# Writing out the opening of a spectral and gated kernel in a fixed order

## The chip, the cores and the metric

The kernel runs on one core of a Trainium2 chip. The metric is the device time of one execution, in microseconds (us). The kernel before was timed in three runs; their median is 1420.48 us (1419.91 to 1420.74). A difference of under 0.2% of that, 2.84 us, is about what a measurement of this kernel cannot tell from no change.

The engines are named as the profile names them: PE (matrix products and transposes), PEld (its weight loads), DVE (the vector engine), ACT (the scalar engine), POOL, and SP, whose queue issues most transfers. Each engine works off its own list of instructions strictly in order and waits for others at semaphores.

## The reference

The input is one activation of 2048 rows by 576 columns. A layer norm is taken over the columns; then the output is the sum of the input, a filter in the two-dimensional Fourier domain, and a gated linear unit:

```
xn = _layernorm(x, axis=-1)
return x + _A_ref(xn, A_w_r, A_w_i) + _B_ref(xn, B_w_gate, B_w_up, B_w_down)
```

where `_A_ref` is `irfft2(rfft2(x) * (w_r + i w_i))`, and `_B_ref` is `h = sigmoid(x @ w_gate) * (x @ w_up)` followed by `h @ w_down`. The gate and up matrices are 576 by 4608, the down matrix is 4608 by 576. This change touches only the first part of the gated unit: the layer norm of the first 1024 rows, their transposes, and the first few products with the gate and up weights.

## The kernel before, in words

**Number format.** [...] A product of 288 columns of depth is written as seven PE instructions (`STEPS`, L630, in `prod`, L634): for each of the two full 128-row pieces of the depth high×high, low×high and high×low, and one for the 32 columns that are left over, whose high, high and low copies are stacked in 96 rows. High parts are made on ACT by a copy, low parts on DVE by a subtraction.

**Tiling of the gated unit.** The 576 columns are two halves of 288, called 1 and 2. The rows are taken in two pairs of chunks of 512 rows; a chunk is four row tiles of 128. `A11`, `A12` are the two column halves of the first chunk of the pair, `A21`, `A22` those of the second; `XA` gives each its place in the tile `X`, which holds them transposed. The 4608 hidden columns are 36 units of 128. From the third unit on, `unit` computes both chunks with seven products in the manner of Strassen, out of sums of these blocks (`S1` to `S4`, made by `sums` and transposed by `fill`). The first two units, whose sums are not ready yet, are computed plainly: `plain(u, c)` (L648) is one call, for unit `u` and chunk `c`, with four products of seven instructions, two into a gate bank and two into an up bank. There are four such calls for the first pair of chunks, in the order (0,0), (1,0), (0,1), (1,1); below they are calls one to four.

**Banks.** The gate bank of unit 0 is called `A` and that of unit 1 `B`; each has one buffer, so call three cannot write bank `A` before the sigmoid of call one (L659) has read it. The up bank `E` has two buffers. Transposes go through `pair` tiles (tag `pp`, two buffers of two halves each).

**The layer norm.** `moments` (L356) takes mean and variance of a row tile on DVE. `scales` (L362) forms the reciprocal root: a square root on ACT, a reciprocal and one refining step in small DVE instructions of two to four columns. `prep_hi` (L405) writes the normalised row tile `xa` on ACT. `fill` (L431) transposes, for one block and two row tiles, the two full pieces and the left-over columns together (four and two PE instructions), copies both out of the bank on ACT (L443, L444), and subtracts for the low part on DVE (L445).

**What sets the order.** The program is built by a scheduler which puts each engine's instructions in order by the sequence of the code and its own estimate of when operands are ready. `placed` (L233) nails an instruction to the sequence of the code while `late_input` is set, which it is up to the end of call four. Side work stands in generators: `second_chunk` (L949) is the weights of unit 1 and the transposes of the second chunk, advanced a few steps at each turn of the plain calls and finished after call one.

**The opening before.** SP issues four row tiles, both halves of unit 0's weights, two row tiles, unit 1's weights, two row tiles (L877 to L880). Meanwhile PE multiplies an identity by itself (L892, L910), which computes nothing that is used. Then come the statistics and transposes of row tiles 0 and 1, those of 2 and 3, the weights of unit 0 (`make_p`, L274), and the statistics of the second chunk's four row tiles in one go (L919).

```
    for k in ("A11", "A12"):
        fill(0, k, 0)
    for n in range(4):
        tc.keep_in_program_order(nc.tensor.matmul(b0, idr, eye, start=False, stop=True, skip_group_check=True))
    for m in (2, 3):
        prep(0, m, 0)
    next(mk)
    next(mk)
    for k in ("A11", "A12"):
        fill(0, k, 1)
```

## Time and profile before

| what | value |
|---|---|
| median of three runs | 1420.48 us (1419.91 to 1420.74) |
| time of the profiled execution | 1421.62 us |
| its span, first to last instruction | 1419.8 us |
| PE busy | 1405.9 us, 99% of the span |
| DVE busy | 1112.5 us, 78% |
| ACT busy | 640.6 us, 45% |
| first product with real weights | 17.01 us after the start |
| first product with the down weights | 63.22 us after the start |

A row of the timeline gives start and length in us, engine, line, operation, what is written and what is read, and how many were merged; in brackets stand the idle time of the engine before it and what ended it. A length runs to the end of the last instruction's pipeline, so that the distance between the starts of two rows of PE is the better measure of PE's own time. PEclk is the clock granted to PE, 1.00 for the full one.

### The profile page before, as it was taken

Reading aid. Unit: us, or ns where it says so; the run is one execution under the profiler, and the core shown is the slowest. Engines: PE = TensorE matmul, PEld = TensorE weight load, DVE = VectorE, ACT = ScalarE, POOL = GpSimd, SP = SyncE. Lnnn points to the kernel's source line nnn. Section 1 sums busy time; section 2 is a strip of 40 time slices with the busy share of each in tenths; the row PEclk is TensorE's granted clock in tenths of the full one; section 3 lists DMA queues with packets and bytes.
Section 4 is the critical chain, followed back from the end, with each engine's and each line's share of the span. In section 5 each row is a group of like instructions: output and inputs, shape, how many; then the busy total and the mean of one; then the engine's idle time right before and its main releaser. Section 6 shows DMA issues by size and latency. Waiting matters only on the chain. (4 is left out here: it accounts for less than half of the span.)

```text
span 1419.8 us, 20725 instructions
## 1 busy us (share of the span) xinstructions
PE 1405.9 (99%) x7883; PEld 1235.9 (87%) x7883; DVE 1112.5 (78%) x1722; ACT 640.6 (45%) x1035; POOL 3.3 (0%) x5
## 2 busy tenths in 40 slices
PE   8999999999999999999999999999999999999998
PEld 6888888888888888888888888888888889999897
DVE  6988888888888888789466888877878877766784
ACT  5644444444444443444235444434545534434431
POOL 0000000000000000000000000000000000000000
PEclk9999999999999999999999999999999999999999
DMA  6498677777777776675767777778888787766643
GB/s 250 181 329 308 256 267 262 270 263 270 263 269 263 269 263 247 242 254 176 270 217 234 224 234 223 217 245 267 275 269 272 236 290 221 247 215 204 195 126 84
DMA packets 130899, 343.10 MB, mean 242 GB/s; under 512 B 12176, under 2 KB 51632, under 8 KB 125936
## 3 DMA queue, kind: packets, MB, share of 16 engines
q1 hardware_dynamic: 129872, 340.47, 71.0%
q8 instruction: 62, 1.02, 0.3%
q10 hardware_dynamic: 928, 1.31, 0.3%
q14 instruction: 37, 0.30, 0.1%
HBM read 205.60 MB, written 136.13 MB: 241 GB/s over the span
## 5 line engine op out<-in xcount | busy, mean ns | idle before, releaser
L636 PE MATMUL pB<-X,w 128*128 128x512 f32 x1484 | 379.9, 393 | 0.0
L636 PEld LDWEIGHTS pB<-X,w 128*128 128x128 f32 x1484 | 268.0, 188 | 49.6 <-ACT v L700 1.3
L636 PE MATMUL pE<-X,w 128*128 128x512 f32 x1064 | 271.8, 392 | 0.5 <-DVE y L701 0.5
L636 PE MATMUL pA<-X,w 128*128 128x512 f32 x1008 | 261.4, 395 | 1.2 <-DVE X L445 0.8
L636 PEld LDWEIGHTS pE<-X,w 128*128 128x128 f32 x1064 | 193.2, 188 | 35.4 <-DVE y L701 1.0
L636 PEld LDWEIGHTS pA<-X,w 128*128 128x128 f32 x1008 | 184.5, 190 | 35.4 <-DVE X L445 1.7
L743 PE MATMUL po<-wd,hh 128*128 128x288 f32 x1216 | 210.8, 295 | 0.0
L834 PEld LDWEIGHTS ps<-wf,hs 128*128 128x128 f32 x1260 | 188.9, 188 | 17.9 <-ACT qs L842 0.9
L834 PE MATMUL ps<-wf,hs 128*128 128x288 f32 x1260 | 202.0, 295 | 0.4 <-ACT qs L842 0.4
L743 PEld LDWEIGHTS po<-wd,hh 128*128 128x128 f32 x1216 | 184.2, 188 | 11.8 <-ACT hh L726 0.4
L747 DVE TENSOR_TENSOR acc<-acc,po 128x576 f32<-128x576 f32 x168 | 125.7, 749 | 67.3 <-PE po L743 66.8
L240 ACT ACTIVATE w<-raw 128x768 fp32r<-128x768 f32 (+1 forms) x106 | 100.8, 952 | 93.1 <-PE pE L636 36.5
L743 PE MATMUL po<-wd,hl 128*128 128x288 f32 x608 | 128.7, 293 | 0.0
L844 DVE TENSOR_TENSOR qs<-qs,ps 128x576 f32<-128x576 f32 x112 | 84.1, 751 | 28.4 <-PE ps L834 27.4
L743 PEld LDWEIGHTS po<-wd,hl 128*128 128x128 f32 x608 | 98.7, 189 | 0.0
L701 DVE TENSOR_TENSOR y<-v,pE 128x512 f32<-128x512 f32 x68 | 46.7, 686 | 52.2 <-ACT v L700 51.3
L844 DVE TENSOR_TENSOR acc<-acc,ps 128x576 f32<-128x576 f32 x90 | 67.5, 750 | 23.3 <-PE ps L834 22.6
L242 DVE TENSOR_TENSOR w<-raw,w 128x512 fp32r<-128x512 f32 (+1 forms) x106 | 81.8, 772 | 3.2 <-ACT w L240 2.9
L721 DVE TENSOR_TENSOR y<-y,g 128x1024 f32<-128x1024 f32 x67 | 81.9, 1222 | 3.1
L770 ACT ACTIVATE hs<-y 128x512 fp32r<-128x512 f32 x105 | 64.8, 628 | 38.2 <-DVE y L721 14.6
L704 ACT ACTIVATE g<-pB 128x512 f32<-128x512 f32 x68 | 40.7, 598 | 89.9 <-PE pB L636 89.9
L700 ACT ACTIVATE v<-pB 128x512 f32<-128x512 f32 x68 | 40.6, 598 | 71.0 <-PE pB L636 70.7
(175 smaller groups left out, 1609.0 us busy)
## 6 DMA issues: line engine op xcount, KB each, us to landing
w<-wsp SPq DMA_DIRECT2D x246, 320.0 KB, 3.5
wsp<-w SPq DMA_DIRECT2D x34, 2240.0 KB, 7.8
raw<-in_w SPq DMA_DIRECT2D x34, 768.0 KB, 9.7
wdsp<-wd SPq DMA_DIRECT2D x36, 576.0 KB, 4.6
wf<-tsp SPq DMA_DIRECT2D x60, 288.0 KB, 3.9
wf<-wdsp SPq DMA_DIRECT2D x45, 288.0 KB, 3.9
std<-in_wd SPq DMA_DIRECT2D x36, 288.0 KB, 5.5
ri<-in_ri SPq DMA_DIRECT2D x16, 578.0 KB, 5.3
```

The source lines that it names most:

```text
L240: placed(nc.scalar.activation(o[:, :, :3, :], src, AF.Copy))
L242: placed(nc.vector.tensor_tensor(o[:, :, 3:, :], src[:, :, :KT, :], f32(o[:, :, :KT, :]), op=OP.subtract))
L636: nc.tensor.matmul(bank, w[:, sw, :], X[:, x, sx, :], start=start and j == 0, stop=stop and j == len(STEPS) - 1, skip_group_check=skip)
L700: nc.scalar.activation(v[:, 1], bank["B"], AF.Copy)
L701: nc.vector.tensor_tensor(y[:, 1], v[:, 1], bank["E"], op=OP.add)
L704: nc.scalar.activation(g[:, 1], bank["B"], AF.Sigmoid)
L721: nc.vector.tensor_tensor(y, y, g, op=OP.mult)
L743: nc.tensor.matmul(pd[:, b, :HD], h[i], w[k][b], start=g == 0 and n == 0, stop=g == G - 1 and n == 2)
L747: nc.vector.tensor_tensor(a, a, pd[:, :, :HD], op=OP.add)
L770: nc.scalar.activation(hs[:, 0], src, AF.Copy)
L834: nc.tensor.matmul(pd[:, i, :HD], h[:, a, m], w[:, b], start=q == 0, stop=q == 2)
L844: nc.vector.tensor_tensor(o, o, pd[:, :, :HD], op=OP.add)
```

## The change

The opening is written as one function, `opening`, which is called in place of plain calls one and two; nearly all its instructions are `placed`. It does the following.

- **Transfers.** The order on SP becomes two row tiles, the gate half of unit 0's weights, two row tiles, the up half, two row tiles, both halves of unit 1's weights, two row tiles.
- **Statistics.** The square root reads the variance itself and gets the small constant as its bias, so that one small DVE step before it and one after it go. The second chunk's statistics are taken two row tiles at a time, as the first chunk's are.
- **Weights first.** ACT copies the gate half of unit 0's weights ahead of the first normalised row tile.
- **Transposes apart.** The full pieces (`lift`) of `A11` and `A12` are transposed together for two row tiles. The left-over columns (`lift_rem`) of all four row tiles go later, four PE instructions for a block and one copy of 512 columns on ACT.
- **Left-overs last.** In calls one and three (`plain_late`) the six instructions of a product that need full pieces alone are issued first (`LOW_LAST`), and the four that need left-over columns stand at the end. The transposes of the left-over columns stand between.
- **Second chunk inside call two.** The row tiles of the second chunk are normalised and transposed between the products of call two.
- **Sigmoids.** The sigmoid of call one moves from the middle of call one to the end of call two, behind all square roots of the opening.
- **Identity products.** There are 15, then 10; before there were 21, ten of full height and eleven more of which eight are of half height in pairs, and then 4.

The new functions and the order, cut:

```diff
+    for todo in ((new_acc, 0, 0), (new_acc, 0, 1), (load_raw, 0, 2), (new_acc, 0, 2), (new_acc, 0, 3), (load_raw, 0, 0),
+                 (new_acc, 0, 4), (new_acc, 0, 5), (load_raw, 1, 2), (load_raw, 1, 0), (new_acc, 0, 6), (new_acc, 0, 7)):
+        todo[0](*todo[1:])
...
-        nc.vector.tensor_scalar(ve, mv[:, ts, 1], EPS, None, op0=OP.add)
         if table:
-            nc.scalar.activation(w0, ve, AF.Sqrt)
-            nc.vector.reciprocal(r0, w0)
+            placed(nc.scalar.activation(w1, mv[:, ts, 1], AF.Sqrt, bias=nmr[:, NT - 1:]))
+            placed(nc.vector.tensor_scalar(ve, mv[:, ts, 1], EPS, -0.5, op0=OP.add, op1=OP.mult))
+            placed(nc.vector.reciprocal(r0, w1))
...
+    def lift(k, mm, main):
+        for j in range(2):
+            for q in range(KT):
+                placed(nc.tensor.transpose(main[:, (2 * q + j) * P:(2 * q + j + 1) * P],
+                                           XS[2 * mm + j][:, XP[k], q * P:(q + 1) * P], idf))
+        v, o = main.rearrange("p (q s) -> p q s", q=KT), X[:, XA[k], :, 2 * mm * P:(2 * mm + 2) * P]
+        return (lambda: placed(nc.scalar.activation(o[:, :KT], v, AF.Copy)),
+                lambda: placed(nc.vector.tensor_tensor(o[:, KT + 1:], v, f32(o[:, :KT]), op=OP.subtract)))
+    def lift_rem(k, ms, rest, srcs=None):
+        for j, m in enumerate(ms):
+            src = srcs[j] if srcs else XR[m, XP[k]]
+            placed(nc.tensor.transpose(rest[:KR, j * P:(j + 1) * P].bitcast(F32R), src, idr))
+        o = X[:KR, XA[k], KT, ms[0] * P:(ms[-1] + 1) * P]
+        return lambda: placed(nc.scalar.activation(o, rest[:KR, :len(ms) * P], AF.Copy))
...
+    LOW_LAST = ((0, 0), (1, 1), (0, 3), (1, 4), (3, 0), (4, 1))
...
+    def plain_late(u, c, beside, mid):
+        G_, bank = new_plain(u, c)
...
+            prod(bank[b], *of_plain(u, c, b, k), k == 1, False, steps=LOW_LAST)
...
+                prod(bank[b], *of_plain(u, c, b, k), False, k == 2, steps=STEPS[-1:])
+            if b == 0 and (u, c) != (0, 0):
+                gate(G_, bank)
...
+    def opening():
...
+        identity(15)
+        scaled(0, 0)
+        early(0, 2)
+        level(0, 0)
+        scaled(0, 1)
+        p1 = pair("px_A11")
...
+        hi_and_lo("A11", 0, p1[:, 0], lows)
+        hi_and_lo("A12", 0, p2[0], lows)
+        identity(10)
+        level(0, 1)
...
+        first = plain_late(0, 0, lambda i: None, mid)
...
+        for k in (1, 2):
+            prod(bank[0], *of_plain(1, 0, 0, k), k == 1, k == 2)
+        lows = []
+        p4 = pair("px_A2_0")
+        for n, k in enumerate(("A21", "A22")):
+            hi_and_lo(k, 0, p4[:, n], lows)
+        scaled(1, 1)
+        level(1, 1)
...
+        p5 = pair("px_A2_1")
+        for n, k in enumerate(("A21", "A22")):
+            hi_and_lo(k, 1, p5[:, n], lows)
+        prod(bank[1], *of_plain(1, 0, 1, 2), False, True, steps=STEPS[4:])
...
+        for m in range(TPC):
+            rem_hi(m, 2, "rm34", TPC)
+            rem_lo(m, 2)
...
+        gate(*first)
+        plain_ends(0, 0, *first)
+        while ends:
+            end()
+        gate(G_, bank)
+        plain_ends(1, 0, G_, bank)
...
+            if p == 0 and n == 2:
+                plain_ends(u, c, *plain_late(u, c, beside, rest_of_second))
```

Three places show what this does to the order on the engines. In the rows `xa` is a normalised row tile, `raw` weights as loaded and `w` their parts, `px_` a bank with transposes, `rs` the small tiles of the statistics, `rm` and `rma` left-over columns, `pA`, `pB`, `pE` the banks of the plain calls, `g` a sigmoid, `y` and `hh` the product with it and its high part. A row says for which engine's semaphore it waits.

First, ACT at the start. Before, from the first square root on:

```order
L368 ACTIVATE rs0_230<-rs0_230 128x2 [waits DVE_49]
L410 ACTIVATE xa0_0_218<-acc_163,nmr_65,rstd_64 128x576 [waits DMAHW1_49,DVE_49,Activation_49]
L410 ACTIVATE xa0_1_219<-acc_163,nmr_65,rstd_64 128x576 [waits DMAHW3_49]
L392 ACTIVATE rma0_0_0_240<-xa0_0_218 128x2x64 [waits Activation_49]
L392 ACTIVATE rma0_1_0_243<-xa0_1_219 128x2x64 [waits Activation_49]
L368 ACTIVATE rs2_255<-rs2_255 128x2 [waits DVE_49]
```

The same place on ACT with the change:

```order
L356 ACTIVATE rs0_225<-mv_63,nmr_65 128x2 [waits DVE_49]
L241 ACTIVATE w0_200<-raw0_182 128x2x384 [waits DMAHW4_49]
L398 ACTIVATE xa0_196<-acc_163,nmr_65,rstd_64 128x576 [waits DMAHW1_49,DVE_49,Activation_49]
L398 ACTIVATE xa1_197<-acc_163,nmr_65,rstd_64 128x576 [waits DMAHW3_49]
L356 ACTIVATE rs2_244<-mv_63,nmr_65 128x2 [waits DVE_49]
```

The weights' copy, with its wait for a transfer, moved ahead of the first normalised row tile, and the left-over columns moved away from here.

Second, ACT around the sigmoid of call one. Before, from the square root of the second chunk:

```order
L368 ACTIVATE rs4_340<-rs4_340 128x4 [waits DVE_49]
L240 ACTIVATE w1_360<-raw1_189 128x2x384 [waits DMAHW2_49]
L659 ACT_TABLE_LOAD
L659 ACTIVATE g0_0_349<-pA0_0_351 128x512 [waits PE_49]
L240 ACTIVATE w1_360<-raw1_189 128x2x384 [waits DMAHW3_49]
L410 ACTIVATE xa0_0_218<-acc_163,nmr_65,rstd_64 128x576 [waits DMAHW0_49,DVE_49]
```

With the change, from the second square root of the second chunk:

```order
L356 ACTIVATE rs6_413<-mv_63,nmr_65 128x2 [waits DVE_49]
L398 ACTIVATE xa2_198<-acc_163,nmr_65,rstd_64 128x576 [waits DMAHW4_49,DVE_49]
L398 ACTIVATE xa3_199<-acc_163,nmr_65,rstd_64 128x576 [waits DMAHW5_49]
L418 ACTIVATE X_66<-px_A2_1_436 128x2x256 [waits PE_49] x2
L381 ACTIVATE rm340_2_452<-xa0_196 128x2x64 [waits Activation_49]
L381 ACTIVATE rm341_2_455<-xa1_197 128x2x64 [waits Activation_49]
L381 ACTIVATE rm342_2_458<-xa2_198 128x2x64 [waits Activation_49]
L381 ACTIVATE rm343_2_461<-xa3_199 128x2x64 [waits Activation_49]
L646 ACT_TABLE_LOAD
L646 ACTIVATE g0_0_308<-pA0_0_309 128x512
L652 ACTIVATE hh0_466<-y0_0_465 128x512 [waits DVE_49]
L646 ACTIVATE g1_0_355<-pB1_0_356 128x512
```

The table load and the sigmoid of call one moved from ahead of the second chunk's row tiles to behind them, their transposes' copies and four copies of left-over columns.

Third, PE from the second chunk's last transposes into call three. Before:

```order
L440 MATMUL px0_A22_1_438<-idr_62,rma0_2_2_421 96x128
L439 MATMUL px0_A22_1_438<-idf_61,xa0_3_221 128x128 x2
L440 MATMUL px0_A22_1_438<-idr_62,rma0_3_2_425 96x128
L636 MATMUL pA0_1_492<-X_66,w0_296 128x512 [waits Activation_49]
L636 MATMUL pE0_1_493<-X_66,w0_296 128x512
L636 MATMUL pA0_1_492<-X_66,w0_296 128x512 [waits DVE_49]
```

With the change:

```order
L415 MATMUL px_A2_1_436<-idf_61,xa3_199 128x128 [waits Activation_49]
L415 MATMUL px_A2_1_436<-idf_61,xa3_199 128x128
L415 MATMUL px_A2_1_436<-idf_61,xa2_198 128x128 [waits Activation_49]
L415 MATMUL px_A2_1_436<-idf_61,xa2_198 128x128
L415 MATMUL px_A2_1_436<-idf_61,xa3_199 128x128 x2
L627 MATMUL pE1_0_357<-X_66,w1_201 128x512 x3
L627 MATMUL pA0_1_479<-X_66,w0_200 128x512 [waits Activation_49]
```

The third row of these is the first transpose of `A22`: it writes the second half of the pair tile whose first half ACT is copying out, and waits for that copy. The wait of the last row is for the sigmoid of call one, which reads bank `A`. The four transposes for the left-over columns of `A21` and four for `A22` (tile `px_r2`) follow twelve instructions later, and those of `A22` in the same way wait for the copy of `A21`'s, which stands on ACT behind the sigmoids of calls one and two.

## The prediction

> **What bounds the kernel now.** I read the page's busy times first, then the stages of the opening as windows, then PE's, ACT's and DVE's timelines row by row.

> ```profile
> span 1419.8 us, 20725 instructions
> PE 1405.9 (99%) x7883; PEld 1235.9 (87%) x7883; DVE 1112.5 (78%) x1722; ACT 640.6 (45%) x1035; POOL 3.3 (0%) x5
> ```

> PE is busy but for 13.9 us in all (1419.8 - 1405.9). What follows the opening is the same work in before and after, and PE has no slack there that could swallow a delay: whatever the opening gains or loses on PE stays to the end. So I forecast when PE reaches one fixed point, the first product with the down weights. The windows, with busy times, then the granted clock, DMA share and GB/s, are those from the start to the first product, call one, call two, and calls three to six.

> ```profile
> 0.00:17.01 17.01, 11.48 (x49) 7.86 (x49) 8.58 (x34) 8.81 (x19) 3.29 (x5) 0.97 0.76 274
> 17.01:26.64 9.63, 9.19 (x29) 7.05 (x29) 8.57 (x27) 4.32 (x8) 0.00 (x0) 0.70 0.61 219
> 26.64:36.59 9.95, 9.61 (x55) 7.55 (x53) 8.66 (x22) 8.42 (x20) 0.00 (x0) 1.00 0.60 213
> 44.28:63.22 18.94, 18.49 (x101) 15.13 (x100) 18.05 (x33) 15.47 (x30) 0.00 (x0) 1.00 0.52 197
> ```

> The first holds 5.5 us without work for PE (17.01 - 11.48), and the second runs at a mean clock of 0.70. There is the gain to be had; call two has only 0.34 us of idle time to lose.

> ```profile
> 3.80 7.44 PE L892 MATMUL b<-idr 128*128 128x512 f32 x21 [3.80 <-DMA idr<-c_id]
> 11.08 0.60 PE L439 MATMUL px_A<-idf,xa 128*128 128x128 f32 x4
> ...
> 14.48 0.66 PE L439 MATMUL px_A<-idf,xa 128*128 128x128 f32 x4 [1.14 <-ACT xa L410]
> ...
> 17.01 0.79 PE L636 MATMUL pA<-X,w 128*128 128x512 f32 x1
> 18.24 5.38 PE L636 MATMUL pA<-X,w 128*128 128x512 f32 x13 [0.43 <-DVE X L445]
> 23.46 3.34 PE L636 MATMUL pE<-X,w 128*128 128x512 f32 x14
> 26.64 3.34 PE L636 MATMUL pB<-X,w 128*128 128x512 f32 x14
> ...
> 37.04 3.25 PE L636 MATMUL pA<-X,w 128*128 128x512 f32 x13 [0.37 <-DVE X L445]
> ...
> 41.49 0.38 PE L439 MATMUL px_S<-idf,xa 128*128 128x128 f32 x2
> 41.62 0.30 PE L440 MATMUL px_S<-idr,rma 128*96 128x128 f32 x1
> ...
> 44.28 3.40 PE L636 MATMUL pB<-X,w 128*128 128x512 f32 x14
> ...
> 55.49 0.44 PE L439 MATMUL px_S<-idf,xa 128*128 128x128 f32 x2 [0.45 <-DVE X L445]
> ```

> A product takes 0.227 us at full clock ((26.64 - 23.46) / 14) and 0.40 at half ((23.46 - 18.24) / 13, its last ones being faster). A transpose takes 0.065 ((41.62 - 41.49) / 2). Why the products from 18.24 are slow, stretches of 3.41 us show:

> ```profile
> 9.22:12.63 3.41, 3.41 (x23) 2.32 (x22) 1.51 (x11) 1.25 (x6) 0.00 (x0) 1.00 1.04 410
> 12.63:16.04 3.41, 1.72 (x12) 1.02 (x11) 1.80 (x4) 3.41 (x9) 0.00 (x0) 1.00 0.59 223
> 16.04:19.46 3.42, 2.94 (x11) 1.92 (x10) 3.05 (x5) 2.62 (x6) 0.00 (x0) 0.50 0.00 0
> 19.46:22.87 3.41, 3.41 (x10) 2.64 (x9) 3.27 (x11) 0.00 (x0) 0.00 (x0) 0.50 0.71 285
> 33.11:36.52 3.41, 3.07 (x20) 2.10 (x18) 3.41 (x10) 2.56 (x8) 0.00 (x0) 1.00 0.61 236
> ```

> One stretch at 50% busy (1.72 of 3.41) is followed by half clock; a stretch at 86% (2.94) did not bring it back, a full one did; one at 90% did not lower it. Half clock therefore came in portions of 3.41 us, at least two of them here.

> **The change, part by part.** The rows that carry the terms on ACT, DVE and the queues:

> ```profile
> 7.67 1.62 ACT L410 ACTIVATE xa<-acc,nmr,rstd 128x576 f32<-128x576 f32 x2 [1.07 <-DVE nmr L382]
> ...
> 12.06 0.60 ACT L443 ACTIVATE X<-px_A 128x512 fp32r<-128x512 f32 x1 [2.14 <-PE px_A L440]
> ...
> 15.47 0.84 ACT L240 ACTIVATE w<-raw 128x768 fp32r<-128x768 f32 x1
> ...
> 24.96 1.28 ACT L659 ACT_TABLE_LOAD   x1
> 26.25 0.60 ACT L659 ACTIVATE g<-pA 128x512 f32<-128x512 f32 x1
> ...
> 29.00 0.50 ACT L392 ACTIVATE rma<-xa 128x128 fp32r<-128x128 f32 x2
> ...
> 33.60 0.64 ACT L664 ACTIVATE hh<-y 128x512 fp32r<-128x512 f32 x1
> ...
> 49.69 0.85 ACT L240 ACTIVATE w<-raw 128x768 fp32r<-128x768 f32 x1 [1.38 <-DVE raw L264]
> ```

> ```profile
> 4.17 0.82 DVE L359 BATCH_NORM_STATS2 st<-acc 128x6 f32<-128x288 f32 x2 [3.30 <-DMA acc<-in_x]
> ...
> 6.63 0.17 DVE L369 RECIPROCAL rs<-rs 128x2 f32<-128x2 f32 x1 [0.27 <-ACT rs L368]
> ...
> 7.42 0.16 DVE L382 SCALAR_TENSOR_TENSOR nmr<-mv,rstd 128x2 f32<-128x2 f32 x1
> ...
> 26.91 0.69 DVE L663 TENSOR_TENSOR y<-g,pE 128x512 f32<-128x512 f32 x1 [0.65 <-ACT g L659]
> ```

> ```profile
> 0.74 1.83 SPq L348 DMA_DIRECT2D acc<-in_x  x4
> 2.62 0.91 SPq L228 DMA_DIRECT2D raw<-in_w  x2
> DMA to landing us min/median/max: 6.1/7.1/8.0
> ```

> *First product.* ACT's new copy of the gate weights stands ahead of the first normalised row tile and waits for a transfer. That is issued after two row tiles instead of four, at about 1.7 (0.74 + 1.83 / 2). If it lands in its own median of 7.1 it is there at 8.8; if it takes only as long as the first row tile, 3.43 us (4.17 - 0.74), at 5.1. With half as much ahead of it I take about 6.5: the copy (0.84) then ends by 7.4, when the scales are ready anyway (7.58 less one removed DVE step, 0.17). The normalising of two tiles (1.62) ends near 9.2; 15 identities at 0.35 (7.44 / 21) hold PE to about 9.8; eight transposes and two copies of 0.6 that overlap a little bring ACT to 11.45, the second two tiles to 13.07, their first transposes and copy the first product to 14.2. With the late landing everything is 1.1 later, 15.3. Before: 17.01.

> *Call one.* 28 products at 0.227 are 6.35; eight left-over transposes 0.6; the second four write the other half of the tile that ACT is copying out, so PE waits for a copy, 0.6 and its start, 0.85. 14.2 + 7.8 = 22.0 against 26.64: a lead of 4.6, of which some 2 is the half clock of before that a quicker start would avoid.

> *Call two* is where the lead goes. Its 28 products are 6.35 us for PE, but between them now stands a chain that PE, ACT and DVE pass to and fro. The gate half, 14 products, ends at 25.2. Then: transposes of `A21`, copy, transposes of `A22` (PE waits 0.85), copy, to 27.7; square root 0.2 and DVE's small steps 0.95 (6.63 to 7.58), to 28.85; two tiles normalised, 1.62, to 30.5; again transposes, copy, wait, transposes, copy, to 32.9; four left-over copies at 0.2 (0.50 less the pipeline's end, for two), to 33.65; the table load, 1.28, to 34.9; the sigmoid of call one, to 35.5. Call three's first product writes bank `A`, so it waits for that sigmoid: 35.55 instead of 36.59 (37.04 less two products). PE's last product of call two ends near 32.75, so the wait is 2.8 us, and the lead is down to 1.0. Before, the table load and the sigmoid lay beside call one's up products (24.96 and 26.25, against 23.46 to 26.64).

> *Call three.* Twelve products (2.7) and four transposes later, at 38.6, PE waits for ACT's copy of the first left-over tile, which stands behind `hh` of call one, the sigmoid of call two, a left-over copy and `hh` of call two: 0.69 + 0.64 + 0.60 + 0.3 + 0.69 + 0.64 + 0.6 = 4.2 after the sigmoid, at 39.9 with starts. That is 1.35 of waiting. 28 products, the left-overs' 0.6, the side transposes of some 1.1 and this wait put call four's start at 45.0; before it is 44.28. A lag of 0.7.

> *Calls four to six.* Up to 63.22 PE waits only 0.45 before. Now the last left-over part of the sums comes behind the copy of unit two's weights, which itself waited 1.38 for DVE before. So the additional wait is between -0.45 (none left) and 1.4; I take 1.0, nearest to the row of 1.38. Lag 1.7.

> *Clock.* From 29.4 to 35.5 PE has only three products and eight transposes, and is busy for about a quarter of the time. Wherever the stretches of 3.41 us lie, one falls into it wholly or nearly so, at well under the 50% that lowered the clock before. Half clock then begins between 32.8 and 36.2 and holds for two portions, 6.83 us. At most this loses 6.83 x (1 - 0.227 / 0.40) = 3.0; the 1.35 of waiting in call three hides part: 1.6 at least. I take 2.0.

> Costed at nothing: the later issues on SP (unit 1's weights and the spills of weight parts, which PE reaches long after; cover: call one), POOL, the left-over copies grouped in fewer (0.37 eight times to 0.6 four times, a gain of 0.6 on ACT that already stands in the times above), the identities, 25 instead of 25. If unit 1's weights came late, call two would begin later than 22.0, and the chain with it.

> Sum: 0.7 + 1.0 + 2.0 = 3.7 us. The profiled execution took 1421.62, 1.1 above the median of 1420.48; 1421.62 + 3.7 = 1425.3, and for the median 1424.2.

> **Rivals.** *The clock stays full:* 1.7 alone, 1422.2. For it: only one stretch in before shows the drop, and the long wait is 2.8 us, not a whole stretch. Against it: that one was half busy, and this is emptier. [...]

> *The clock also falls early,* between the transposes of the start or in call two's first group, where PE is about 75 to 80% busy, between the 50% that lowered it and the 90% that did not: another 2.3, since part of it lies beside waits: 1426.5.

> *Faster:* the sigmoid of call one is off the path. If the chain through call two runs 2.8 us quicker (left-over copies and table load in ACT's waits for PE, done by 32.75), call three starts with the products' end, the clock has no reason to fall and the lead of 3.8 stays but for call three's wait: 3.7 - 2.8 - 2.0 = -1.1. ACT's backlog there and in the calls after would be gone too, since it stems from the late sigmoid: without 1.35 and 1.0 it is -3.4, so 1417.1. To break even the sigmoid must be done near 33.8, with the clock up. Against it: on ACT the sigmoid stands behind all of the chain, each link of which has a row above.

> **How the numbers follow.** A measurement tells no less than 0.2%, 2.84 us. Forecast 0.51 (of it 0.35 over that bound, 0.16 within); clock stays 0.16 (0.13 within, 0.03 slower); clock falls early too 0.18 (0.17 slower, 0.01 within); sigmoid off the path 0.12 (0.08 faster, 0.04 within); anything else 0.03 (0.02 slower, 0.01 faster). Faster 0.09, same 0.34, slower 0.57. The range: downwards the steady clock with no later wait, 0.7 - 0.45 = 0.25, so 1420.7; upwards the late weights, the greatest wait and clock loss, 0.7 + 1.1 + 1.4 + 3.0 = 6.2, and a little of the early clock: 1427.5.

> **What would show it.** Right: first product near 14.2; call three's first gate product near 35.5 with some 2.8 us idle before it, released by the sigmoid of call one, and the table load at about 33.6; PE idle before the transposes of `A22`, released by ACT's copy; the clock at 0.50 for about 6.8 us between 33 and 43; the first down product near 67. Wrong: call three before 33, or a full clock throughout, or a first down product ahead of 63.

## The result and the profile after

The changed kernel takes 1424.66 us (median of 7 runs, 1424.23 to 1425.41) against 1420.48 (7 runs, 1419.68 to 1421.04): a ratio of 1.0031, with a 95% interval of 1.0019 to 1.0042. It is 4.2 us slower, more than the bound of 2.84 us, although the lower end of the interval, 2.7 us, lies just under that bound. The forecast was 1424.2.

The page of the changed kernel, then its stages as windows: to the first product, call one, call two, call three, calls four to six.

```profile
span 1422.4 us, 20721 instructions
PE 1405.2 (99%) x7883; PEld 1236.1 (87%) x7883; DVE 1112.8 (78%) x1725; ACT 640.4 (45%) x1032; POOL 3.3 (0%) x5
```

```profile
0.00:14.09 14.09, 10.23 (x42) 8.18 (x42) 8.20 (x30) 7.78 (x13) 3.29 (x5) 1.00 0.86 322
14.09:22.08 7.99, 7.30 (x36) 5.96 (x37) 6.41 (x21) 4.80 (x11) 0.00 (x0) 1.00 0.61 176
22.08:35.89 13.81, 9.18 (x46) 6.60 (x44) 9.52 (x31) 8.50 (x15) 0.00 (x0) 1.00 0.53 212
35.89:46.65 10.76, 10.08 (x48) 8.17 (x49) 7.58 (x20) 5.21 (x12) 0.00 (x0) 0.84 0.00 0
46.65:66.77 20.12, 18.88 (x102) 15.08 (x101) 18.42 (x33) 15.97 (x32) 0.00 (x0) 1.00 0.57 222
```

The opening does begin sooner: the first product comes at 14.09 instead of 17.01, and call one takes 7.99 at full clock instead of 9.63. Then call two takes 13.81 instead of 9.95, with 4.6 us in which PE has nothing to do (13.81 - 9.18), and call three runs at a mean clock of 0.84. The places where PE waits, from its timeline:

```profile
14.09 3.04 PE L627 MATMUL pA<-X,w 128*128 128x512 f32 x12 [0.25 <-ACT X L418]
...
19.43 0.48 PE L424 MATMUL px_r<-idr,rm 128*96 128x128 f32 x4 [0.69 <-ACT X L426]
...
22.08 3.34 PE L627 MATMUL pB<-X,w 128*128 128x512 f32 x14
...
26.55 0.66 PE L415 MATMUL px_A<-idf,xa 128*128 128x128 f32 x4 [0.69 <-ACT X L418]
...
31.84 0.66 PE L415 MATMUL px_A<-idf,xa 128*128 128x128 f32 x4 [0.69 <-ACT X L418]
...
35.89 4.61 PE L627 MATMUL pA<-X,w 128*128 128x512 f32 x12 [2.70 <-ACT g L646]
...
41.43 0.48 PE L424 MATMUL px_r<-idr,rm 128*96 128x128 f32 x4 [0.68 <-ACT X L426]
...
46.65 3.45 PE L627 MATMUL pB<-X,w 128*128 128x512 f32 x14
...
55.05 0.27 PE L424 MATMUL px_S<-idr,rma 128*96 128x128 f32 x1 [1.19 <-DVE rma L386]
...
66.77 0.69 PE L764 MATMUL po<-wd,hh 128*128 128x288 f32 x4
```

The largest is 2.70 us, released by the sigmoid of call one (`g`, L646). Behind what that sigmoid stands, ACT's timeline tells; from 27.73 on its rows come in the order of ACT's list, as it stands with the change:

```profile
32.54 0.60 ACT L418 ACTIVATE X<-px_A 128x512 fp32r<-128x512 f32 x1 [0.74 <-PE px_A L415]
33.03 0.90 ACT L381 ACTIVATE rm<-xa 128x128 fp32r<-128x128 f32 x4
33.94 1.28 ACT L646 ACT_TABLE_LOAD   x1
35.23 0.60 ACT L646 ACTIVATE g<-pA 128x512 f32<-128x512 f32 x1
```

Bank `A` was complete at about 21.8 (its last two products begin at 21.18 and last 0.61), and its sigmoid begins at 35.23. The first row writes the high part of a block, fp32r from float32; a low part is what DVE's subtraction (L419) leaves. Stretches of 3.41 us on either side of the wait:

```profile
29.44:32.85 3.41, 2.17 (x13) 1.28 (x11) 1.58 (x4) 2.13 (x4) 0.00 (x0) 1.00 0.19 78
32.85:36.27 3.42, 0.72 (x4) 0.34 (x3) 3.10 (x10) 2.95 (x7) 0.00 (x0) 1.00 0.00 0
36.27:39.68 3.41, 3.41 (x10) 2.64 (x9) 3.41 (x9) 1.76 (x4) 0.00 (x0) 0.50 0.00 0
```

PE was 21% busy (0.72 of 3.42) in the middle one, and the next ran at half clock. So the lead over the kernel before reads: 4.56 us at call two (26.64 - 22.08), 0.70 at call three (36.59 - 35.89), then a lag of 2.37 at call four (46.65 - 44.28) and of 3.55 at the first down product (66.77 - 63.22).

### The profile page after: what moved, and what is told of

It is laid out like the page before. It is cut to its first block, busy times and chain, and to the rows that moved or that the text cites. A ratio compares the mean times of both kernels' runs of the same rounds, so it can differ in the third digit from the quotient of the medians.

```text
span 1422.4 us, 20721 instructions
## 1 busy us (share of the span) xinstructions
PE 1405.2 (99%) x7883; PEld 1236.1 (87%) x7883; DVE 1112.8 (78%) x1725; ACT 640.4 (45%) x1032; POOL 3.3 (0%) x5
## 3 DMA queue, kind: packets, MB, share of 16 engines
q8 instruction: 62, 1.02, 0.3%
```

## The experiments

Each run was timed beside runs of the kernel before, whose medians were 1420.48 for the changed kernel, 1420.70 for the next four rows, and 1420.43 or 1420.44 for the rest; so a difference of two medians in this table can be off by some 0.3 us. "Start of call three" is the first product into bank `A` of chunk two.

| kernel | median us | ratio to before, 95% interval | start of call three | first down product |
|---|---|---|---|---|
| the changed kernel | 1424.66 | 1.0031 (1.0019 to 1.0042) | 35.89 | 66.77 |
| sigmoid early | 1418.99 | 0.9989 (0.9980 to 0.9997) | 32.74 | 62.06 |
| ten identities in the wait | 1423.36 | 1.0019 (1.0010 to 1.0028) | 35.95 | 65.81 |
| statistics in one go | 1423.74 | 1.0022 (1.0013 to 1.0031) | 34.70 | 66.68 |
| tiles apart | 1422.47 | 1.0014 (1.0005 to 1.0023) | 34.29 | 65.03 |
| sums ahead of weights | 1424.93 | 1.0032 (1.0019 to 1.0044) | 36.48 | 67.20 |
| all together | 1414.69 | 0.9962 (0.9949 to 0.9974) | 29.69 | 57.03 |
| kernel before, filled | 1419.70 | 0.9995 (0.9986 to 1.0005) | 35.54 | 62.18 |
| weights later | 1424.70 | 1.0031 (1.0020 to 1.0042) | 36.32 | 66.20 |
| sigmoid early, sums ahead | 1418.22 | 0.9985 (0.9976 to 0.9994) | 32.59 | 60.67 |
| three identities in the wait | 1424.31 | 1.0026 (1.0015 to 1.0036) | 36.17 | 67.06 |

For the kernel before, filled, the start is that of the main part, less two products that run ahead of it, as in the prediction. The start of call two, up to which most of these kernels are alike, lies between 21.89 and 22.74 in their traces, so a distance between two rows of one trace says more than a start alone.

### The sigmoid of call one, early

```diff
-        for m in (0, 1):
+        for m in range(TPC):
             moments(acc[TPC + m], TPC + m, R["pool"])
         next(W[1, 2])
-        scales(TPC, 2, R["pool"], True)
+        scales(TPC, TPC, R["pool"], True)
+        gate(*first)
+        plain_ends(0, 0, *first)
+        end()
         level(1, 0)
...
-        scaled(1, 1)
         level(1, 1)
...
-        gate(*first)
-        plain_ends(0, 0, *first)
         while ends:
```

> The changed kernel, but the second chunk's statistics are taken in one go (one square root for four row tiles) and the table load and the sigmoid of call one stand right behind that square root, ahead of the second chunk's row tiles, with the product y behind it. Theory (call three waits for the sigmoid because that ends a serial chain of 34 us on ACT): the wait of 2.70 us before call three's first product goes, that product starts at about 32 instead of 35.9, the clock stays at 1.00. Of the 4 us some 2 are given back before the first down product, where unit two's weights and the sums are late next: the first down product at about 61.5 (66.8 changed, 63.2 before), the time about 1419.4, which would be below the kernel before. Rival A (ACT and DVE are behind by as much anyway, the sigmoid is only where it shows): call three starts no earlier than 35, time within 1 us of 1424.7. Rival B (nothing is given back later): first down product at 59.5 to 60, time 1417 to 1418.

PE's timeline of this kernel:

```profile
32.74 2.98 PE L627 MATMUL pA<-X,w 128*128 128x512 f32 x12
...
41.91 3.41 PE L627 MATMUL pB<-X,w 128*128 128x512 f32 x14
...
50.30 0.27 PE L424 MATMUL px_S<-idr,rma 128*96 128x128 f32 x1 [1.23 <-DVE rma L386]
...
62.06 0.69 PE L764 MATMUL po<-wd,hh 128*128 128x288 f32 x4
```

The row of call three's start has no wait any more, the clock stays full, and the kernel is 5.7 us faster than the changed one: 1418.99, where 1419.4 was expected. It is 1.7 faster than the one before, with an interval clear of no change but less than the bound of 2.84. The edit also takes the second chunk's statistics in one go; against the kernel below that does only this, the sigmoid's place is worth 4.8 us (1423.74 - 1418.99). So it carries most of the loss, and the rival of an ACT and a DVE that are as late anyway is refuted. The lead over before shrinks from 3.85 at call three (36.59 - 32.74) to 2.37 at call four (44.28 - 41.91) and 1.16 at the first down product (63.22 - 62.06), much as expected; the last step is the wait of 1.23 for the sums' left-over part.

### Ten identity products in the wait, and three

```diff
         prod(bank[1], *of_plain(1, 0, 1, 2), False, True, steps=STEPS[4:])
+        fl = pair("fl")[:, 0].rearrange("p (a s) -> p a s", a=4)
+        for n in range(10):
+            placed(nc.tensor.matmul(fl, idr, eye, start=n == 0, stop=True, skip_group_check=True))
```

> The changed kernel with ten identity products more, written ahead of call three's first product, where PE waits 2.70 us for the sigmoid; they compute nothing that is used and end before the wait does. Theory (the emptiness of this stretch, 21% busy, lowers the clock for the next 3.41 us; its price is 12 products at 0.37 instead of 0.227, 1.7 us, of which part lay beside a wait of ACT's copy in call three that now gets longer, 0.68 to about 1.3): the clock stays 1.00 throughout, call three still starts at 35.9, the first down product about 1.1 earlier, time about 1423.6. Rival A (the clock's fall costs all that it slows): 1.7 less, 1422.9 or below. Rival B (it costs nothing, since ACT is the bound there): unchanged, 1424.7, with the wait in call three at 2.2 or more.

PE's timeline with the ten:

```profile
35.95 3.02 PE L627 MATMUL pA<-X,w 128*128 128x512 f32 x12 [0.41 <-ACT g L646]
...
40.46 0.48 PE L424 MATMUL px_r<-idr,rm 128*96 128x128 f32 x4 [1.24 <-ACT X L426]
```

Call three starts as late as before the edit, but its twelve products take 3.02 instead of 4.61 us, and the wait for ACT's copy grows from 0.68 to 1.24. The time falls by 1.3 us, to 1423.36, or by 1.5 if each kernel is taken against the runs of before beside it; 1423.6 was expected. So the clock's fall was not free. In the window from 30.00 to 35.95 the granted clock is 1.00, and behind it the products take 0.25 each (3.02 / 12) and not 0.38 (4.61 / 12). In the traces the fall cost 1.0 at the first down product (66.77 - 65.81), less than the 1.6 by which the products were longer, as part of that lay beside the wait; the medians alone do not tell 1.3 to 1.5 from 1.6.

With three of them (`range(3)`), 0.7 us of the 2.7:

> The changed kernel with three instead of ten identity products ahead of call three's first product, 0.7 us of the 2.7 us wait. In the profiled runs so far, a stretch of 3.41 us with two to three products and at most four transposes, or two products and eight transposes, was followed by half clock, one with three products and six transposes or more was not. Theory (what counts is how much PE did in a stretch, not whether it was idle without a break): five products in the emptiest stretch are enough, the clock stays 1.00, time as with ten, 1423.4. Rival (an unbroken idle time of about 2 us within a stretch is what lowers it): half clock for 3.4 to 6.8 us after 36, time 1424.0 to 1425.

```profile
33.19:36.60 3.41, 1.39 (x7) 0.85 (x6) 3.16 (x10) 2.90 (x7) 0.00 (x0) 1.00 0.00 0
36.60:40.01 3.41, 3.41 (x10) 2.64 (x9) 3.41 (x9) 1.81 (x4) 0.00 (x0) 0.50 0.00 0
```

The windows show the stretch 41% busy (1.39 of 3.41) and half clock behind it. The theory, a full clock with five products in the stretch, is refuted; 1424.31 lies where the rival put it. But the rival's reason, an unbroken idle time of about 2 us, does not hold either: in the kernel before, the stretch from 12.63 has no gap over 1.14 and the clock fell, and with the weights' copy later (below) the stretch from 34.50 begins with 1.82 of idle time (36.32 - 34.50) and it did not.

### Statistics of the second chunk in one go

The sigmoid stays at the end of call two.

```diff
-        for m in (0, 1):
+        for m in range(TPC):
             moments(acc[TPC + m], TPC + m, R["pool"])
         next(W[1, 2])
-        scales(TPC, 2, R["pool"], True)
+        scales(TPC, TPC, R["pool"], True)
...
-        scaled(1, 1)
         level(1, 1)
```

> The changed kernel, but the second chunk's statistics are taken in one go; the sigmoid of call one stays at the end of call two. It takes one square root and one row of small DVE steps, about 1.3 us, out of the chain through call two. Theory (the chain is serial and on the path): call three starts at 34.6 instead of 35.9, time between 1422.6 (clock stays full) and 1423.7 (it falls). Rival (the four row tiles' statistics on DVE delay unit 1's low parts and with them call two, 1.9 us): call two's first product later than 22.1 by up to 1.5 and no gain, 1424.7 or more.

PE's timeline, and the stretches from the windows:

```profile
34.70 5.49 PE L627 MATMUL pA<-X,w 128*128 128x512 f32 x12 [2.69 <-ACT g L646]
```

```profile
30.52:33.94 3.42, 1.35 (x7) 0.88 (x7) 1.96 (x7) 2.65 (x7) 0.00 (x0) 1.00 0.28 117
33.94:37.35 3.41, 2.65 (x6) 2.15 (x7) 3.41 (x10) 2.01 (x5) 0.00 (x0) 0.50 0.00 0
37.35:40.76 3.41, 3.26 (x11) 2.26 (x9) 2.73 (x7) 0.74 (x2) 0.00 (x0) 0.50 0.00 0
```

Call three starts at 34.70, 1.2 earlier, but still waits 2.69 for the sigmoid, since the products of call two end sooner too. In this execution the half clock lasted two stretches and not one: the first of them was only 78% busy (2.65 of 3.41). The median, 1423.74, is at the edge of what was expected for a falling clock. The chain is on the path; one square root and one row of small steps are worth 0.9 us of time.

### Tiles apart

```diff
-        p4 = pair("px_A2_0")
-        for n, k in enumerate(("A21", "A22")):
-            hi_and_lo(k, 0, p4[:, n], lows)
+        for k in ("A21", "A22"):
+            hi_and_lo(k, 0, pair(f"px_{k}_0")[:, 0], lows)
```

and the same for `p5`.

> The changed kernel, but the second chunk's transposes of A21 and A22 go to tiles of their own, so that those of A22 need not wait for ACT's copy of A21's (0.69 us at 26.55 and again at 31.84). Theory (both waits lie in the serial chain): call three starts about 1.7 earlier, at 34.2, time about 1421.8 if the clock stays full, 1423 if it falls. Rival (the chain is held by ACT and DVE, not by these waits): call three moves by less than 0.7, time 1424.2 or more.

```profile
34.29 4.49 PE L627 MATMUL pA<-X,w 128*128 128x512 f32 x12 [2.73 <-ACT g L646]
```

PE's timeline has call three at 34.29, where 34.2 was expected, and the waits at 26.55 and 31.84 are gone. The time, 1422.47, lies between the two cases of the clock, of which both occur: the five runs with a mean granted clock of 1.000 have a median of 1421.69, and the two with 0.998 took 1422.70 and 1422.93, where 1421.8 and 1423 were expected. So both waits were in the chain.

### The sums ahead of unit two's weights

```diff
+        if late_input[0]:
+            sides[:] = [g for g in sides if next(g, sides) is not sides]
         for _ in range(n):
             next(make, None)
         next(wd, None)
         while adds:
             adds.pop(0)()
-        sides[:] = [g for g in sides if next(g, sides) is not sides]
+        if not late_input[0]:
+            sides[:] = [g for g in sides if next(g, sides) is not sides]
```

> The changed kernel, but in each turn up to the end of call four the sums' side work (row sums, their left-over parts, their transposes) is written ahead of unit two's weights instead of behind them. Theory (the wait of 1.19 us at 55.05, which PE has for the last left-over part of S1's second half, comes from standing behind the copies and subtractions of unit two's weights on ACT and DVE): the wait goes, the first down product about 1.2 earlier, time about 1423.5. Rival (DVE is simply short of time there, so that unit two's weights are late instead): a wait of the same size before the third unit's first product, no gain, 1424.7.

The wait of 1.19 is gone from PE's timeline; what stays is the wait that the kernel before has too:

```profile
48.32 3.40 PE L627 MATMUL pB<-X,w 128*128 128x512 f32 x14
...
59.33 0.66 PE L415 MATMUL px_S<-idf,xa 128*128 128x128 f32 x4 [0.45 <-DVE X L419]
...
67.20 0.69 PE L764 MATMUL po<-wd,hh 128*128 128x288 f32 x4
```

From call four to the first down product it takes 18.88 us (67.20 - 48.32), as before the change (18.94), where the changed kernel takes 20.12. But the time, 1424.93, did not fall: this was a miss. In the profiled run the half clock lasted two stretches in place of one, and four of its five runs had a mean granted clock of 0.997, against 0.998 to 0.999 in the runs of the changed kernel. So the same edit was made where the clock does not fall, on top of the early sigmoid:

> The sigmoid of call one early and the second chunk's statistics in one go, and the sums' side work ahead of unit two's weights: here the clock stays full, so that the second edit shows by itself, which it did not on the changed kernel (1424.93, with two portions of half clock in the profiled run against one). Theory (the wait for the sums' left-over part costs 1.2 us on PE, of which 0.6 remain as the wait that the kernel before has there too): 0.7 to 1.2 below the sigmoid early alone (1418.99), 1417.8 to 1418.3. Rival (DVE and ACT are short of time there, what is won is given back in the third unit): 1418.9 or more.

```profile
41.77 3.40 PE L627 MATMUL pB<-X,w 128*128 128x512 f32 x14
...
60.67 0.69 PE L764 MATMUL po<-wd,hh 128*128 128x288 f32 x4
```

PE's timeline gives 18.90 for the same distance (20.15 without the edit), and the time is 1418.22, 0.77 below the early sigmoid alone, within what was expected; 0.3 of that is the difference of the runs of before. By itself the edit came with the longer half clock:

```profile
32.32:35.73 3.41, 1.35 (x7) 0.88 (x7) 1.97 (x7) 2.65 (x7) 0.00 (x0) 1.00 0.00 0
35.73:39.15 3.42, 2.67 (x6) 2.15 (x7) 3.42 (x10) 2.00 (x5) 0.00 (x0) 0.50 0.00 0
39.15:42.56 3.41, 3.25 (x11) 2.26 (x9) 2.72 (x6) 0.76 (x2) 0.00 (x0) 0.50 0.00 0
```

The first stretch ends 0.75 us ahead of call three (36.48), as in the kernel with the statistics in one go (0.76, 34.70 - 33.94), where the half clock also lasted two stretches; in the changed kernel it ends 0.38 behind call three's start (36.27 - 35.89), and the half clock lasted one. So a different lie of the stretches fits the profiled run. Why four of five runs had it was not settled.

### The kernel before, with its first gap filled

```diff
-    for n in range(4):
+    for n in range(8):
         tc.keep_in_program_order(nc.tensor.matmul(b0, idr, eye, start=False, stop=True, skip_group_check=True))
```

> The kernel before, with eight identity products instead of four after the first transposes; they compute nothing that is used and lie in its wait of 1.14 us before 14.48. Theory A (of the changed kernel's lead of 4.6 at call two some 3 are the clock that does not fall in call one, but such a lead is worth little without earlier statistics and transposes of the second chunk): the clock stays 1.00 through call one, the first product stays at 17.0, call two's first product is some 1.5 to 3 earlier, and call three starts only about 1 earlier; time about 1419.3. Rival B (all that the clock gives stays): 3 us, 1417.6. Rival C (the stretch of 50% busy is not what lowers the clock): clock 0.50 for two portions as before and 1420.5.

```profile
12.43:15.84 3.41, 2.64 (x13) 1.72 (x13) 1.77 (x4) 3.41 (x9) 0.00 (x0) 1.00 0.73 270
15.84:19.25 3.41, 2.27 (x13) 1.63 (x14) 2.85 (x6) 2.85 (x6) 0.00 (x0) 1.00 0.00 0
```

```profile
24.99 3.88 PE L636 MATMUL pB<-X,w 128*128 128x512 f32 x14 [0.28 <-ACT w L240]
...
35.99 3.24 PE L636 MATMUL pA<-X,w 128*128 128x512 f32 x13 [0.38 <-DVE X L445]
```

The windows have that stretch 77% busy now (2.64 of 3.41), and the clock stays at 1.00 behind it. On PE's timeline call two begins 1.65 earlier (26.64 - 24.99), call three only 1.05 (37.04 - 35.99), and the time is 1419.70, 0.7 lower, with an interval that takes in no change. A faster call one is thus worth little by itself, as expected. PE's lead over before, 2.08 us at call one's up products (23.46 - 21.38), is lost at unit 1's weights: PE waits 0.28 for ACT's copy, and call two's first 14 products take 3.72 us (28.71 - 24.99) instead of 3.17 (29.81 - 26.64), with a wait of the weight loads for DVE's part among them. ACT's copy stands behind the square root of the second chunk's statistics:

```profile
23.99 0.21 ACT L368 ACTIVATE rs<-rs 128x4 f32<-128x4 f32 x1 [5.30 <-DVE rs L366]
```

That square root comes no sooner than in the kernel before (24.00), since DVE's statistics do not.

### The weights' copy, later

```diff
-        early(0, 2)
         level(0, 0)
...
         level(0, 1)
-        next(W[0, 2])
+        early(0, 2)
...
         hi_and_lo("A12", 1, p2[1], lows)
+        next(W[0, 2])
         for lo in lows:
```

> The changed kernel, but ACT copies the gate half of unit 0's weights only after the normalising of row tiles 2 and 3, and their low parts are taken on DVE after the transposes' low parts. The first product then waits for weights copied at about 13.7. Theory (the earlier first product, 14.1 against 17.0, comes from the transposes standing apart and from the statistics' shorter way, the weights being first is worth what their copy takes in ACT's queue less PE's wait there): first product 0.2 to 0.4 later, call three and all behind it as much later, time 1425.0. Rival (the weights being first carries most of the 2.9 us): first product at 15.5 or later, time 1426 or more.

```profile
14.01 1.20 PE L627 MATMUL pA<-X,w 128*128 128x512 f32 x4 [0.34 <-ACT X L418]
15.43 2.11 PE L627 MATMUL pA<-X,w 128*128 128x512 f32 x8 [0.22 <-DVE X L419]
...
36.32 3.02 PE L627 MATMUL pA<-X,w 128*128 128x512 f32 x12 [2.70 <-ACT g L646]
```

PE's first product is no later, where 0.2 to 0.4 was expected. After four products PE waits for DVE, and from the first product to call two it takes 8.51 us (22.52 - 14.01) instead of 7.99; call three is 0.4 later, and the time, 1424.70 (1423.40 to 1425.83), cannot be told from that of the changed kernel. So "weights first" does not carry most of the 2.9 us; it is worth about 0.5, and in call one. In this profiled run the clock did not fall.

### All together

The early sigmoid, the tiles apart, the sums ahead of the weights, and also:

```diff
-                p3 = pair("px_r1")
-                for n, k in enumerate(("A11", "A12")):
-                    lift_rem(k, range(TPC), p3[:, n])()
+                for k in ("A11", "A12"):
+                    lift_rem(k, range(TPC), pair(f"px_r{k}")[:, 0])()
```

and the same for `px_r2`.

> The changed kernel with all its new waits taken out together: the sigmoid of call one early with the second chunk's statistics in one go, own tiles for the transposes of A21 and A22 and for the left-over transposes of both chunks, and the sums' side work ahead of unit two's weights. Theory (the waits lie one behind the other on PE: 2.9 before call three, 0.9 at each of four places for ACT's copy of the other half of a tile, 1.4 for the sums' left-over part): 4.6 us below the kernel with the sigmoid early alone (1419.0), so about 1414.4, clock full throughout, first down product at about 57. Rival (a wait taken out comes back at the next place, since ACT and DVE set the pace through calls two to four): 1416.5 to 1418, with PE waiting for DVE or ACT before call three or in the third unit.

```profile
14.22 3.02 PE L627 MATMUL pA<-X,w 128*128 128x512 f32 x12 [0.25 <-ACT X L418]
...
21.32 3.34 PE L627 MATMUL pB<-X,w 128*128 128x512 f32 x14
...
29.69 2.90 PE L627 MATMUL pA<-X,w 128*128 128x512 f32 x12
...
49.14 0.66 PE L415 MATMUL px_S<-idf,xa 128*128 128x128 f32 x4 [0.46 <-DVE X L419]
...
57.03 0.69 PE L764 MATMUL po<-wd,hh 128*128 128x288 f32 x4
```

It takes 1414.69, 10.0 us less than the changed kernel and 5.7 less than the one before (0.9962, 0.9949 to 0.9974); 1414.4 was expected. On PE's timeline call two takes 8.37 us (29.69 - 21.32). From the sigmoid early with the sums ahead to this kernel there are only the four half-tile waits, and they are worth 3.5 us (1418.22 - 1414.69), about 0.9 each. Here, what was won at one wait was not given back at the next.

## Why the prediction was right

**First product and call one.** Forecast 14.2 and 22.0, measured 14.09 and 22.08. The trace shows ACT's weight copy free of its wait by 6.27, near the 6.5 assumed.

```profile
6.27 0.84 ACT L241 ACTIVATE w<-raw 128x768 fp32r<-128x768 f32 x1
```

```profile
3.61 6.18 PE L910 MATMUL b<-idr 128*128 128x512 f32 x15 [3.61 <-DMA idr<-c_id]
...
10.41 2.56 PE L910 MATMUL b<-idr 128*128 128x512 f32 x10
```

The hit at 14.2 has luck in it. 15 identities at 0.35 from 3.80 end at 9.05 and not at the 9.8 that the prediction goes on with; they ended at 9.62, because they took 0.40 each, where the ten after them took 0.24 (12.80 - 10.41). The 0.35 was a mean over a row that mixes full and half height.

**Call two.** This step carried the forecast: a chain through ACT at whose end the sigmoid of call one holds bank `A`. Forecast 35.55 with a wait of 2.8, measured 35.89 with 2.70. The early sigmoid takes it away, and with it the loss; tiles apart and statistics in one go bring call three forward by about their terms, 1.6 and 1.2.

**Call three.** The wait for ACT's copy was forecast as 1.35 and measured as 0.68. The term was right for a full clock (1.24 with ten identities), but PE, at half clock, came to the place later.

**Calls four to six.** An addition of 1.0 was forecast, 1.18 measured (20.12 - 18.94). Its place was the one named, the sums' left-over part behind unit two's weights; moving it is worth 0.5 to 0.8 of time where the clock does not interfere.

**Clock.** That it falls was right, and that the empty stretch before call three is its cause too: with ten identities in it (4.50 us busy of the 5.95 up to call three) the twelve products behind it took 3.02 us and not 4.61. The size was off: two stretches of half clock were forecast, 2.0 us; the profiled run had one, from 36.27 to 39.68, which was fully busy (3.41 of 3.41), and with ten identities the cost came out as 1.3 to 1.5 in the medians and 1.0 at the first down product. This is the term of the sum that was mis-sized.

**Sum.** 3.7 forecast, 3.55 measured at the first down product. That this is so close is in part luck: the clock cost 1.0 less than forecast there, while call three began 0.3 late, and without the clock (ten identities) call three and calls four to six took 0.3 and 0.2 longer than forecast. In the medians it is 4.2, between the two profiled executions 2.6 (1424.23 - 1421.62): that of before took longer than any of its seven timed runs, that of after was the shortest of its seven. That nothing is given back after the first down product holds to within 1 us between these two traces: the lag of 3.55 there is 2.6 at the end (1422.4 - 1419.8). Which waits give that back was not tried.

**Rivals.** The steady clock was priced at 1422.2; with the clock held the time is 1423.36. The 1.2 between are small parts: call three began 0.4 later than forecast (35.95), calls three and four to six each took 0.2 to 0.3 longer, and its runs of before were 0.2 higher. The faster case, the sigmoid off the path, was priced at 1417.1 and came to 1418.99, because two later waits stayed that this price had taken away with it: 0.69 in call three for ACT's copy (at 36.66 in its trace), and the 1.23 for the sums' left-over part.

In the changed kernel the half clock lasted 3.41 us (36.27 to 39.68), in the kernel before 6.83 (16.04 to 22.87), two such stretches. The stretch ahead of the fall was not idle: 21% busy here (0.72 of 3.42), 41% with three identities (1.39 of 3.41), 50% in the kernel before (1.72 of 3.41).

## What to carry to other kernels

Before bringing work forward, follow the consumer of each single-buffered bank: the sigmoid that was moved to the end of call two on ACT kept bank `A` until 35.23, though its input was ready at about 21.8, and moving it back up was worth 4.8 us. Two halves of one tile, one being copied out while the other is written, cost a wait of about 0.9 us each time here (3.5 us for four, 0.69 of it as PE's idle time in a trace); tiles apart took that wait away. An early lead is worth what the next stage can take over: filling the gap of the kernel before gave call two 1.65 us and the whole kernel 0.7, which its interval does not tell from nothing.

## What the runs showed of the hardware

```profile
31.08:34.50 3.42, 1.78 (x9) 1.08 (x9) 1.36 (x3) 2.13 (x8) 0.00 (x0) 1.00 0.14 57
34.50:37.91 3.41, 1.59 (x7) 1.33 (x8) 3.41 (x12) 2.50 (x4) 0.00 (x0) 1.00 0.00 0
37.91:41.32 3.41, 2.17 (x16) 1.73 (x15) 3.41 (x9) 1.87 (x5) 0.00 (x0) 1.00 0.00 0
```

Busy time includes the ends of pipelines: in the kernel before, the two transposes from 41.49 last 0.38, though the next one begins at 41.62, 0.13 after their start. So many short transposes may count for more in it than for the clock; that is a guess. The next figure of a row, the busy time of the weight loads, does put these stretches in order: 0.34 to 1.02 us where the clock fell, and 1.08 and 1.33 here, or 1.28 in the changed kernel's stretch from 29.44, where it did not. No run was made to test this, and 1.02 and 1.08 lie close, so it is a lead and not a rule; what exactly is measured stays open. Behind a stretch at half clock that was 78% (statistics in one go) or 86% busy (the kernel before, 2.94 of 3.42) the clock stayed at half; behind one of 93% (tiles apart, 3.17 of 3.41) or more it was full again.

The clock's column says 1.00 from the start of the run, but the same identity product took 0.40 us in the row from 3.61 and 0.24 in the row from 10.41. The first is near the 0.40 of a product at half clock in the prediction, so the column is not to be trusted for the first microseconds.

The same program also meets the stretches differently from run to run. Of the 33 runs of the kernel before in the first set, all 15 with a mean granted clock of 0.997 took 1420.6 us or more, and all four with 0.999 or 1.000 took 1419.9 or less: some 1.5 us of its spread goes with the half clock. The one such run whose trace was kept has it in the opening; for the others that is inferred.
